# A gated attention unit followed by hash routing: the first z load, the place of the token load, one drain on GpSimd and the number of turns between two gates

## The chip, the cores and the metric

The kernel runs on one core of a Trainium2 chip. Its time is the device time of one execution in microseconds (us); smaller is better. The core has a matrix engine (PE, with its weight loads PEld), a vector engine (DVE), a scalar engine (ACT), GpSimd (POOL) and a sync engine (SP). SP, ACT and POOL can issue DMAs.

## The reference

Two stages run behind each other. In the first, for each of 8 batches of 2496 rows, with z of 64 columns and u, v of 256 columns:

```python
scores = scale * np.matmul(z, z.transpose(0, 2, 1))      # scale = 1 / 2496
attn = np.maximum(scores, 0.0) ** 2
out = np.matmul(attn, v)
x = u * out                                              # (8, 2496, 256)
```

In the second, each of the 19968 rows of x goes through the expert that its token id names (8 experts, 256 to 1024 to 256 columns):

```python
expert_idx = token_ids * np.int64(2654435761) % np.int64(E)
for e in range(E):
    h = np.maximum(x[expert_idx == e] @ w1[e], 0.0)
    out[expert_idx == e] = h @ w2[e]
```

## The kernel before, in words

**Tiles.** A batch has T = 20 tiles of rows: TM = 19 of 128 rows and one odd tile of 64 rows. A partition holds 19 neighbouring rows, so tile t is row t of each partition. Five groups (NG = 5) of G = 4 tiles form a batch; the last group has three whole tiles and the odd one.

**z.** The scores need z with its 64 columns on the partitions, and they need it twice, in partitions 0 to 63 and 64 to 127, because even and odd tiles use the two halves of PE at the same time (`scores`, line 202). For batch 0, `load_z` (line 121) loads z twice side by side, once from SP and once from ACT, and `turn_z` (line 149) turns each tile with its copy on PE with an identity matrix, four tiles into one PSUM tile, which one ACT copy takes to `zT`. In the later batches DVE turns z instead.

**Scores and squares.** `scores(b, g)` makes the scores of all tiles against the four tiles of group g. ACT and DVE take turns at the relu out of PSUM (batch 0: even tiles ACT, odd tiles DVE). `square(n)` squares the next n of them, on DVE in batch 0, on ACT later. PSUM has six buffers for scores and everything else of `mm_ps`, and two accumulators (`acc_ps`).

**Mirrored batches.** From batch 1 on the symmetry of the scores is used: only some tiles are computed, and DVE turns the others in 32x32 blocks (`turns_of`, line 236, and `own_turns`). These turns stand in a list `to_turn`, and `turn_scores(steps)` (line 275) sends out as many as 1600 elements per step allow, each costing its elements and 170. `turn_now` sends out at once what an attend needs and has not been turned.

**The order.** All of it is written by hand in one loop over the 40 groups (line 589). A group begins with the attends of its first EARLY = 2 tiles, goes on tile by tile (an attend of four matmuls, `square(2)`, `turn_scores(1)`, one small step of the routing by `between`), then makes the scores of the next group, and ends with two halves: the last LATE = 3 tiles for two of the four row tiles, their gates (`gate`, line 332: accumulator times u, on DVE), then `square(2)`, `turn_scores(1)`, `between`. A gate frees the accumulator that the next group begins with.

**Routing.** `places` computes on DVE, in steps between the attends, where each token goes; its first step reads the token ids. POOL then writes each row of x to its slot in DRAM by indirect DMAs.

**The experts.** Behind the loop, `run` (line 706) takes blocks of 256 slots: `up` (matmuls, relu), `down` (matmuls, ACT copy), and `store`, an indirect DMA from POOL. The last two blocks come behind a branch (`tc.If`, line 730) for a token distribution that needs more blocks; POOL issues twelve stores for that case (`later`) in any event, whose indices are out of bounds when the branch is not taken.

**Queues at the start.** SP issues its copy of z(0), V(0) in seven DMAs, u(0,0), and z(1) with V(1). ACT issues the other copy of z(0) and the token ids. POOL makes the constants: a corner of `short`, the identity, index tables, and `zero` (line 358), the source of the DMAs that clear the slots.

Of the kernel before, what the change touches and what calls it, by code (L numbers as in the profile page):

```python
# [10 lines left out]
F32 = mybir.dt.float32  # L11
# [13 lines left out]
def kernel(  # L25
# [59 lines left out]


    short = const.tile([P, T, R], F32)
    nc.gpsimd.memset(short[R:P, TM, :], 0.0)
    odd = const.tile([R, D], F32)
    ident = const.tile([P, P], F32)  # L90
    make_identity(nc, ident[:])

# [25 lines left out]

    def load_z(b):
        if b == 0:
            zn[b] = npool.tile([P, T, 2, K], F32, name="zn")
            for i in range(2):
                tiles_io(zf, b, range(T), zn[b][:, :, i, :], False, nc.scalar if i else nc.sync, twice=True)
            return
        zn[b] = npool.tile([P, T, NQ, Q], F32, name="zn")
        rows = zf[ds(b * S, S), :]
        for q in range(NQ):
            cols = ts(q % 2, Q)  # L130
            o = zn[b][ts(q, Q)]
            for t, m in ((slice(0, TM), rows[0:SM, cols].rearrange("(j i t) k -> i t j k", i=Q, t=TM)),
                         (TM, rows[SM:S, cols].rearrange("(j i) k -> i j k", i=Q))):
                if t == TM:
                    for h in range(2):
                        nc.sync.dma_start(o[:, TM, ds(h * R // Q, R // Q), :], m)
                else:
                    nc.sync.dma_start(o[:, t], m)
# [10 lines left out]
    def turn_z(b, g):  # L149
        if g == 0:  # L150
            zT[b] = zpool.tile([P, T * P], F32, name="zT")
        o = zT[b][:, ts(g, G * P)]
        if b:
            nc.vector.transpose(o, zn[b][:, ts(g, G)].rearrange("p t j k -> p (t j k)"))
            return
        ps = mm_ps.tile([P, G * P], F32, name="z_ps", tag="mm")
        for i, t in enumerate(group(g)):
            nc.tensor.transpose(ps[:, ts(i, P)], zn[b][:, t].rearrange("p h k -> p (h k)"), ident[:])
        nc.scalar.copy(o, ps[:])

    def whole(g):

# [34 lines left out]
    def scores(b, g):  # L197

        n = sum(width(t) for t in group(g))
        for k, t in enumerate(fresh(b, g)):  # L200
            lo = skipped(b, g, t)
            h = ds((t % 2 if t % G < 2 or not mirrored(b) else 1 - t % 2) * K, K)
            ps = mm_ps.tile([P, G * P], F32, name="s_ps", tag="mm")
            nc.tensor.matmul(ps[:, lo:n], zT[b][h, ts(t, P)], zT[b][h, ds(g * G * P + lo, n - lo)], start=True, stop=True)  # L204
            if t % G == 0:
                made[b, g, t // G] = apool.tile([P, G, G * P], F32, name="a", tag="a")
                rooms.append((b, g, t // G))
            a = made[b, g, t // G][:, t % G, lo:n]
            if (k % 8 == 7 and g < 2) if mirrored(b) else k % 2:
                nc.vector.tensor_scalar_max(a, ps[:, lo:n], 0.0)  # L210
            else:
                nc.scalar.activation(a, ps[:, lo:n], AF.Relu)  # L212
            to_square.append((b, g, t))

    def square(n):
        for b, g, t in to_square[:n]:
            a = made[b, g, t // G][:, t % G, :]
            m = len(whole(g)) * P
            lo = skipped(b, g, t)
            pairs = [(a[:, lo:m], a[:, lo:m])] if lo < m else []  # L220
            if m < G * P:
                pairs.append((short[0:width(t), t, :], a[0:width(t), ds(m, R)]))
            for o, x in pairs:
                if mirrored(b):
                    nc.scalar.square(o, x)  # L225
                else:
                    nc.vector.tensor_mul(o, x, x)
            if mirrored(b) and t % G == G - 1:
                turns = turns_of(b, g, t // G) if t // G > g else own_turns(b, g)
                to_turn.extend((n, (b, g, t // G), f) for n, f in turns)  # L230

                to_turn.sort(key=lambda e: min(e[1][2] - g, 2 if fine(g) else 1))
        del to_square[:n]
# [120 lines left out]
    token = const.tile([P, B, T], I32)  # L354

    tok = const.tile([P, B, T, 2], I32)
    zero = const.tile([P, D], F32)
    nc.gpsimd.memset(zero[:], 0.0)
    CLEAR = T // 2
    assert NS % CLEAR == 0  # L360

# [5 lines left out]
    def load_tokens():  # L367
        tok_h = dataclasses.replace(moe_token_ids.tensor, shape=list(moe_token_ids.tensor.shape))
        tok_w = tok_h.bitcast(I32).rearrange("(b s two) -> b s two", b=B, two=2)
        nc.scalar.dma_start(tok[:, :, 0:TM, :], tok_w[:, 0:SM, :].rearrange("b (p t) two -> p b t two", t=TM))  # L370
        nc.scalar.dma_start(tok[0:R, :, TM, :], tok_w[:, SM:S, :].rearrange("b p two -> p b two"))

    def places():

# [144 lines left out]
    def place_x():  # L519
# [5 lines left out]
        tc.declare_no_dep(st.ins, group="x", reason="each token has its own slot")  # L525
        tc.add_to_no_dep_group("x", st.ins)

    order = tc.manual_schedule()
    order.__enter__()

    load_z(0)
    load_v(0)
    load_u(0, 0)
    load_tokens()
    for g in range(NG):
        turn_z(0, g)

# [47 lines left out]
        nc.vector.transpose(xT[j].rearrange("p k h i -> p (k h i)"), xg[j].rearrange("p k d -> p (k d)"))  # L585

    scores(0, 0)
    square(EARLY)
    for n, (b, g) in enumerate(groups):
        if n + 1 < len(groups):  # L590
            load_u(*groups[n + 1])
        if g == 0 and b + 1 < B:
            load_z(b + 1)
            load_v(b + 1)
        if n == NG - 1:
            m = pool("mirror", 1)
            mirrors = [m.tile([P, G, G, P], F32, name=f"m_{k}") for k in range(NG * NG // 4)]

        acc = [acc_ps.tile([P, 2, D], F32, name="acc", tag="acc") for _ in range(2)]
        for k in range(2):  # L600
            for t in range(EARLY):
                attend(b, g, t, acc, [2 * k, 2 * k + 1])
            square(2)
            turn_scores(1)
            between()
        for t in range(EARLY, TM - LATE):
            if g == NG - 1 and b + 1 < B and t % 2 == 0 and t // 2 <= NG:
                turn_z(b + 1, t // 2 - 1)
            if n + 1 == len(groups) and t == T // 4:

                w_buf = list(mirrors)
                w_buf.extend(mirror[b, a, g] for a in range(NG - 1))
                load_w(0, 0)
            if n + 1 == len(groups) and t == T // 2:
                assert not gated
                x_all = vpool.tile([P, T, D], F32, name="v_sb")
                x_bufs = [x_all[:, ts(k, DP * BLK // D), :].rearrange("p c d -> p (c d)") for k in range(2 * LOADS)]
                xg_buf = [x.rearrange("p (k d) -> p k d", d=D // NQ) for x in x_bufs[:LOADS]]
                xT_buf = [x.rearrange("p (k h i) -> p k h i", h=DP, i=Q) for x in x_bufs[LOADS:]]
                for k in range(AHEAD):  # L620
                    load_x(k, k)
            if n + 1 == len(groups) and t >= TM - LATE - AHEAD:
                turn_x(t - (TM - LATE - AHEAD), t - (TM - LATE - AHEAD))
            attend(b, g, t, acc, range(G))
            if t % G == G - 1 and (b, t // G, g) in mirror and g < NG - 1:
                mirrors.append(mirror.pop((b, t // G, g)))
            square(2)
            turn_scores(1)
            between()
        assert not to_square  # L630
        if g == NG - 1:
            gate_short(b, attend_short(b))
            if n + 1 == len(groups):
                load_w(1, 1)
            mirrors.extend(mirror.pop(k) for k in sorted(mirror))
        attend_last(b, g, acc)
        between()
        if n + 1 < len(groups):

            m = len(fresh(*groups[n + 1])) // G  # L640
            for key in rooms[max(0, len(rooms) - NA):max(0, len(rooms) - NA + m)]:
                turn_now(key)
            scores(*groups[n + 1])
        square(3)
        turn_scores(1)

        for k in range(2):
            for t in range(TM - LATE, TM):
                attend(b, g, t, acc, [2 * k, 2 * k + 1])
            for q in (2 * k, 2 * k + 1):  # L650
                gate(b, g, q, acc)
            square(2)
            turn_scores(1)
            between()
        between()
    assert not to_turn and next(place, None) is None and i > 2 * T + 4 * C
# [49 lines left out]
    def run(first, last, loads, later=None):  # L706
# [19 lines left out]
    run(0, NM, NU)  # L726
    n_used = nc.values_load(extra[0:1, 0:1], min_val=1, max_val=NB + N, engines=[
        mybir.EngineType.PE, mybir.EngineType.Activation, mybir.EngineType.DVE, mybir.EngineType.SP])
    later = []
    with tc.If(n_used > NU):  # L730
        for j in [*range(AHEAD), *range(NU, NB)]:
# [37 lines left out]
```

## Time and profile before

| | |
|---|---|
| time, median of 3 runs | 2685.01 us (2684.61 to 2685.49) |
| the profiled execution's own time | 2687.06 us |
| its span, first to last instruction | 2685.1 us |
| PE, weight loads, DVE, ACT, POOL busy | 99%, 84%, 51%, 21%, 18% |
| first matmul starts, last one ends | 9.36 us, 2677.4 us |
| first scores, first attend | 13.79 us, 24.06 us |
| z loads of batch 0 issued | 0.82 us, from SP and ACT |
| token ids issued from ACT, first read on DVE | 4.42 and 8.27 us, 25.73 us |
| last store issued on POOL | 2678.05 us |

The page of a profile gives each engine's busy time and the costliest groups of instructions; the trace behind it can be asked for the waits (which engine waited for which, how long in total, how often, the longest), for a timeline of a window (start, duration, engine, line, operation, out and in, shapes, number, and in brackets the idle time before it with what ended it), for busy times in chosen stretches, and for the instructions of one line, the sequencers' own ones among them. Ends of matmuls are modelled, about 0.38 us behind the start for 256 columns, while the next starts 0.2155 us behind the last. A line number is that of the kernel.

### The profile page before, as it was taken

The numbers are of one execution on the slowest core, as the hardware profiler recorded it, in microseconds if no ns is written. First come the engines' busy times: TensorE is split into PE (matmuls) and PEld (weight loads), VectorE is DVE, ScalarE is ACT, GpSimd is POOL, SyncE is SP. The second block draws the span as 40 slices with busy tenths as digits, with TensorE's granted clock in tenths as the row PEclk, the third lists the DMA queues.
The fourth block names the chain that finished last, engine by engine and source line by source line (L and its number), as shares of the span: only waits on it lengthen the run. The fifth ranks groups of instructions, "written<-read, shape, count | busy, mean of one in ns | idle before, by whom it ended". The sixth has DMA issues, their size and how long they took to land. (4 is left out here: it accounts for less than half of the span.)

```text
span 2685.1 us, 33980 instructions
## 1 busy us (share of the span) xinstructions
PE 2662.1 (99%) x12650; PEld 2255.2 (84%) x12650; DVE 1357.5 (51%) x2813; ACT 567.6 (21%) x1221; POOL 494.2 (18%) x513
## 2 busy tenths in 40 slices
PE   8999999999999999999999999999999999999998
PEld 6877887888888888888878888888888888888887
DVE  6556886887878878878878811111111111111110
ACT  2013314214222233123132111111111111111111
POOL 0221222122212221222101121111111111111113
PEclk9999999999999999999999999999999999999999
DMA  9612113013103122131101287777777777777773
GB/s 295 206 31 74 32 32 89 17 32 89 31 20 87 31 46 62 29 90 32 32 16 32 62 200 188 187 188 193 195 187 190 188 187 186 194 194 192 188 189 88
DMA packets 334842, 308.93 MB, mean 115 GB/s; under 512 B 187308, under 2 KB 293693, under 8 KB 334672
## 3 DMA queue, kind: packets, MB, share of 16 engines
q1 hardware_dynamic: 309424, 264.78, 39.2%
q0 software_dynamic: 21072, 41.10, 5.2%
q8 instruction: 102, 1.67, 0.3%
q10 hardware_dynamic: 4176, 0.82, 0.2%
q14 instruction: 68, 0.56, 0.1%
HBM read 243.25 MB, written 65.70 MB: 115 GB/s over the span
## 5 line engine op out<-in xcount | busy, mean ns | idle before, releaser
L329 PE MATMUL acc<-v_sb,a 128*128 128x256 f32 x3760 | 828.7, 380 | 3.7 <-issue 2.2
L329 PEld LDWEIGHTS acc<-v_sb,a 128*128 128x128 f32 x3760 | 710.3, 190 | 112.5 <-issue 7.9
L241 DVE STREAM_TRANSPOSE m<-a 32x512 f32<-32x512 f32 (+1 forms) x1120 | 756.8, 676 | 17.1 <-issue 0.3
L683 DVE TENSOR_SCALAR hT<-h_ps 128x512 f32<-128x512 f32 x162 | 112.1, 692 | 951.0 <-PE h_ps L675 933.9
L675 PE MATMUL h_ps<-v_sb,m 128*128 128x256 f32 x2592 | 586.0, 379 | 2.2 <-issue 1.1
L688 PE MATMUL o_ps<-m,hT 128*128 128x256 f32 x2592 | 585.2, 379 | 0.0
L675 PEld LDWEIGHTS h_ps<-v_sb,m 128*128 128x128 f32 x2592 | 492.3, 190 | 70.3 <-issue 2.1
L688 PEld LDWEIGHTS o_ps<-m,hT 128*128 128x128 f32 x2592 | 492.5, 190 | 67.0
L329 PE MATMUL acc<-v_sb,m 128*128 128x256 f32 x2016 | 439.7, 379 | 0.0
L329 PEld LDWEIGHTS acc<-v_sb,m 128*128 128x128 f32 x2016 | 383.0, 190 | 52.1
L212 ACT ACTIVATE a<-s_ps 128x512 f32<-128x512 f32 (+3 forms) x442 | 205.7, 578 | 902.9 <-PE s_ps L204 902.9
L522 POOL DMA_INDIRECT x_rows<-x_sb,slot_i x160 | 157.8, 986 | 1075.4 <-DVE x_sb L338 884.8
L700 POOL DMA_INDIRECT out_dram<-o_sb,idx x158 | 153.5, 972 | 918.7 <-ACT o_sb L695 903.8
L695 ACT COPY o_sb<-o_ps 128x256 f32<-128x256 f32 x162 | 60.3, 372 | 741.4 <-PE o_ps L688 737.5
L204 PE MATMUL s_ps<-zT 64*128 64x512 f32 (+5 forms) x1040 | 211.2, 549 | 0.0
L257 DVE STREAM_TRANSPOSE a<-a 32x128 f32<-32x128 f32 (+2 forms) x896 | 201.4, 249 | 7.8
L225 ACT ACTIVATE a<-a 128x512 f32<-128x512 f32 (+3 forms) x413 | 202.1, 625 | 0.0
L204 PEld LDWEIGHTS s_ps<-zT 64*128 64x128 f32 x1040 | 123.9, 187 | 81.8 <-issue 57.2
L510 POOL DMA_INDIRECT slot_tokens<-token,addr x160 | 158.8, 993 | 159.4 <-DVE addr L504 109.1
L681 ACT ACTIVATE hT<-h_ps 128x512 f32<-128x512 f32 x162 | 96.7, 597 | 229.0 <-PE h_ps L675 218.2
L210 DVE TENSOR_SCALAR a<-s_ps 128x512 f32<-128x512 f32 (+1 forms) x78 | 51.4, 659 | 146.6 <-PE s_ps L204 145.5
L338 DVE SCALAR_TENSOR_TENSOR x_sb<-acc,u_sb 128x256 f32<-128x256 f32 x152 | 57.9, 420 | 133.7 <-PE acc L329 132.8
(80 smaller groups left out, 380.6 us busy)
## 6 DMA issues: line engine op xcount, KB each, us to landing
m<-in_moe_w_dram SPq DMA_DIRECT2D x324, 256.0 KB
m<-in_moe_w_dram SPq DMA_DIRECT2D x81, 1024.0 KB
x_rows<-zero SPq DMA_DIRECT2D x10, 2176.0 KB
v_sb<-x_rows SPq DMA_DIRECT2D x324, 64.0 KB
v_sb<-in_v_dram SPq DMA_DIRECT2D x32, 512.0 KB
u_sb<-in_u_dram SPq DMA_DIRECT2D x32, 512.0 KB
zn<-in_z_dram SPq DMA_DIRECT2D x28, 304.0 KB
v_sb<-in_v_dram SPq DMA_DIRECT2D x8, 384.0 KB
```

The lines of the kernel that those rows point to most:

```text
L204: nc.tensor.matmul(ps[:, lo:n], zT[b][h, ts(t, P)], zT[b][h, ds(g * G * P + lo, n - lo)], start=True, stop=True)
L212: nc.scalar.activation(a, ps[:, lo:n], AF.Relu)
L225: nc.scalar.square(o, x)
L241: nc.vector.transpose(mirror[b, a, g][ts(c, Q)].rearrange("p t s q -> p (t s) q")[:, 0:m, ts(r, Q)], made[b, a, g][ts(r, Q)].rearrange("p ...
L257: return n * Q, lambda: nc.vector.transpose(out, in_)
L329: nc.tensor.matmul(acc[i // 2][:, i % 2, :], lhs(b, g, t, i), v_sb[b][:, t, :], start=(k == 0 and i % 2 == 0), stop=(k == TM - 1), skip_gr ...
L510: st = nc.gpsimd.indirect_dma_start(out=slot_dram[:, None], out_offset=bass.IndirectOffsetOnAxis(ap=addr[0:n, c:c + 1], axis=0), in_=token ...
L522: st = nc.gpsimd.indirect_dma_start(out=x_dram[:, :], out_offset=bass.IndirectOffsetOnAxis(ap=slot_i[0:width(c % T), c:c + 1], axis=0), in ...
L675: nc.tensor.matmul(ps[:, i, :], w1[j][:, c, ts(f + i, P)], xT[j][:, :, c, :], start=(c == 0), stop=(c == DP - 1))
L683: nc.vector.tensor_scalar_max(o, ps[:], 0.0)
L688: nc.tensor.matmul(ps[:], hT[j][:, f, ts(t, P)], w2[j][:, f, :], start=(f == 0), stop=(f == FP - 1))
L700: st = nc.gpsimd.indirect_dma_start(out=out[:], out_offset=bass.IndirectOffsetOnAxis(ap=rows, axis=0), in_=o, in_offset=None, bounds_check ...
```

## The change

z of batch 0 is loaded once, from SP, in one piece of 19 rows per partition, with a slot 0 ahead of the tiles that gets a copy of the odd tile on DVE. Turning slots t and t + 1 together puts tile t - 1 in the lower half and tile t in the upper half; DVE copies the upper half to its place, ACT the lower half, one tile further on (for the first group in two pieces, since the odd tile goes to the end). `zero` is the first memset that POOL makes for the kernel; ACT makes a one-element copy of it first of all, and PE five matmuls with it into a PSUM tile that nobody reads. The token ids are loaded from SP, behind V(0) and ahead of u(0,0). In the scores of the very first group, the first two squares are made by ACT behind score 10 instead of by DVE behind score 19. `turn_scores` between the two halves at a group's end gets 0.8 steps instead of 1. POOL gets a drain instruction ahead of the branch to the last blocks.

```diff
     short = const.tile([P, T, R], F32)
-    nc.gpsimd.memset(short[R:P, TM, :], 0.0)
     odd = const.tile([R, D], F32)
+    zero = const.tile([P, D], F32)
+    nc.gpsimd.memset(zero[:], 0.0)
     ident = const.tile([P, P], F32)
     make_identity(nc, ident[:])
+    nc.gpsimd.memset(short[R:P, TM, :], 0.0)
...
         if b == 0:
-            zn[b] = npool.tile([P, T, 2, K], F32, name="zn")
-            for i in range(2):
-                tiles_io(zf, b, range(T), zn[b][:, :, i, :], False, nc.scalar if i else nc.sync, twice=True)
+
+            zn[b] = npool.tile([P, T + 1, K], F32, name="zn")
+            tiles_io(zf, b, range(T), zn[b][:, 1:, :], False, nc.sync, twice=True)
+            nc.vector.tensor_copy(zn[b][:, 0, :], zn[b][:, T, :])
             return
...
         for i, t in enumerate(group(g)):
-            nc.tensor.transpose(ps[:, ts(i, P)], zn[b][:, t].rearrange("p h k -> p (h k)"), ident[:])
-        nc.scalar.copy(o, ps[:])
+            nc.tensor.transpose(ps[:, ts(i, P)], zn[b][:, t:t + 2].rearrange("p t k -> p (t k)"), ident[:])
+        nc.vector.tensor_copy(o[K:P], ps[K:P, :])
+        for i, n in ((0, G), ) if g else ((0, 1), (1, G - 1)):
+            nc.scalar.copy(zT[b][0:K, ds((g * G + i - 1) % T * P, n * P)], ps[0:K, ds(i * P, n * P)])
...
             to_square.append((b, g, t))
-
-    def square(n):
+            if (b, g, t) == (0, 0, T // 2):
+                square(EARLY, nc.scalar)
+
+    def square(n, eng=None):
...
-                if mirrored(b):
+                if mirrored(b) or eng is nc.scalar:
                     nc.scalar.square(o, x)
...
-    zero = const.tile([P, D], F32)
-    nc.gpsimd.memset(zero[:], 0.0)
...
-        nc.scalar.dma_start(tok[:, :, 0:TM, :], tok_w[:, 0:SM, :].rearrange("b (p t) two -> p b t two", t=TM))
-        nc.scalar.dma_start(tok[0:R, :, TM, :], tok_w[:, SM:S, :].rearrange("b p two -> p b two"))
+        nc.sync.dma_start(tok[:, :, 0:TM, :], tok_w[:, 0:SM, :].rearrange("b (p t) two -> p b t two", t=TM))
+        nc.sync.dma_start(tok[0:R, :, TM, :], tok_w[:, SM:S, :].rearrange("b p two -> p b two"))
...
+    WARM = 5
...
+    nc.scalar.copy(odd[0:1, 0:1], zero[0:1, 0:1])
+    warm = mm_ps.tile([P, D], F32, name="warm", tag="mm")
+    for _ in range(WARM):
+        nc.tensor.matmul(warm[:], zero[:, 0:P], zero[:], start=True, stop=True)
     load_z(0)
     load_v(0)
+    load_tokens()
     load_u(0, 0)
-    load_tokens()
...
     scores(0, 0)
-    square(EARLY)
...
             square(2)
-            turn_scores(1)
+            turn_scores(1 if k else 0.8)
             between()
...
         mybir.EngineType.PE, mybir.EngineType.Activation, mybir.EngineType.DVE, mybir.EngineType.SP])
+
+    nc.gpsimd.drain()
     later = []
```

## The prediction, on record before the changed kernel ran

> **What bounds the kernel now.** I read the busy times first, then the waits of the matrix engine (PE), then the timeline where those waits lie.
>
> ```profile
> PE 2662.1 (99%) x12650; PEld 2255.2 (84%) x12650; DVE 1357.5 (51%) x2813; ACT 567.6 (21%) x1221; POOL 494.2 (18%) x513
> ```
>
> PE is busy for 2662.1 of 2685.1 us. The change takes no matmul out of the long loops, so it can only win in the 23 us where PE does not run, or where PE runs slower than it could. The waits of PE say where that is (us in total, times, longest):
>
> ```profile
> PE z_ps L158 <- DMA zn<-in_z_dram: 9.4, 1, 9.4
> PE acc L329 <- issue: 2.2, 7, 0.3
> PE acc L329 <- DVE a L227: 1.4, 1, 1.4
> PE h_ps L675 <- issue: 1.1, 3, 0.4
> PE h_ps L675 <- ACTq L730: 1.0, 1, 1.0
> ```
>
> These are 15.1 us; the rest is the 7.7 us behind the last matmul (2677.4 to 2685.1). Nothing else stands between this kernel and an unbroken matmul stream, so I go through the places that the edits touch.
>
> **The start.** Timeline, 0 to 40 us (start, duration, engine, line, operation):
>
> ```profile
> 0.82 5.47 SPq L113 DMA_DIRECT2D zn<-in_z_dram  x3
> 9.36 4.50 PE L158 MATMUL z_ps<-ident,zn 128*128 128x128 f32 x20 [9.36 <-DMA zn<-in_z_dram]
> 10.48 0.59 ACT L159 COPY zT<-z_ps 128x512 f32<-128x512 f32 x1 [0.25 <-PE z_ps L158]
> 11.33 0.59 ACT L159 COPY zT<-z_ps 128x512 f32<-128x512 f32 x1 [0.27 <-PE z_ps L158]
> 13.79 8.85 PE L204 MATMUL s_ps<-zT 64*128 64x512 f32 x40
> 23.32 2.49 DVE L227 TENSOR_TENSOR a<-a 128x512 f32<-128x512 f32 x4
> 24.06 12.35 PE L329 MATMUL acc<-v_sb,a 128*128 128x256 f32 x56 [1.42 <-DVE a L227]
> ```
>
> (1) The load. z(0) comes twice, in 256-byte pieces, by two queues; the stretches from 3.4 to 9.36 us show 223 to 228 GB/s. Now it comes once, 608 KB in one piece per partition and the odd tile twice at 16 KB: half of the bytes. A long-piece load that stands alone is u at 275.35: 512 KB, data from 276.3, at its end by 279.0, so 3.65 us from its issue, with 287 to 303 GB/s at the end. 640 KB add 128 KB at that rate, 0.45 us: 4.1 us, landing at 0.82 + 4.1 = 4.9. The odd tile's two small loads are issued behind it on SP and land inside that or a little later; the DVE copy that duplicates the odd tile waits for them. 128x64 lies between the rows 64x8 (0.16 us) and 128x152 (0.23 to 0.24 us). The first transpose can start near 5.2. If the small loads trail, 6.5; not before 4.9.
>
> (2) The warm-up. Five 128x256 matmuls are ten passes (the trace shows each fp32 matmul as two). Later passes run at 0.2155 us (48 in 10.52 at 2666.84, less one latency). PE needs `zero`, a 0.32 us memset now first on POOL, so it starts near 1.2 and ends at 3.4; at half pace at 5.5. It stands ahead of the transposes on PE; at worst it costs 0.3 us against the landing. I take 5.5 for the first transpose, 3.9 earlier than now.
>
> (3) The transposes. There are 20 as before. The ACT copies above come every 0.853 us for four transposes, 0.213 us for 128 columns: the price of a 256-column pass later. So they run at half the later pace per column, either because PE's clock is low after 9 idle us or because a transpose has that price. The granted clock in the windows reads 1.00 from 0 on, idle stretches included, so it does not decide. Bounds: 20 x 0.213 = 4.3 us if nothing changes, 20 x 0.107 = 2.1 us if PE is warm. I take a third at the old pace: 7 x 0.213 + 13 x 0.107 = 2.9. They end at 8.4 and, with the 0.33 us that PE loses at the switch, scores start at 8.7 instead of 13.79: **-5.1**; ends -2.7 (6.5 + 4.3 + 0.33 = 11.1) and -6.2 (5.2 + 2.1 + 0.33 = 7.6).
>
> [...]
>
> (4) The copies out of PSUM split: per group 0.69 us on DVE (the 128x512 rows of L210) beside 0.59 us on ACT, ACT with one more for the first group. Five on DVE take 3.5 us and end near 10. The first scores need only groups 0 and 1, ready near 8.0; the later buffers come free ahead of PE. Cost 0. The ACT table load (1.28 us at 8.95, behind ACT's DMA issues) goes to the first us, since ACT issues no DMA any more.
>
> (5) Squares 0 and 1 on ACT. PE waits 1.42 us for the first DVE square (23.32); at the next switch of the same kind (62.61) it waits for nothing. ACT now squares both tiles after score 10: 2 x 0.625 us ahead of the relus of scores 12 to 18. Pair j starts at 8.7 + 0.86j and its relu 1.16 us later (14.95 against 13.79), so score 10 is through ACT at 14.75, the squares at 16.0, score 12 at 16.6. Score 18 (j = 9, 16.4) takes the sixth buffer back, that of score 12: 0.28 us late. **-1.1** (ends -1.45 and -0.5). Next in line are squares 2 and 3 on DVE, due 3.4 us after the first attend and done 2 us after it.
>
> (6) Tokens. On SP behind seven V loads: issued near 7, behind 2.5 MB at 339 to 386 GB/s (30 to 50 us), landed by 14. Their first reader (DVE L400, 25.73 now) comes near 19.5. Cover 5 us; were it gone, DVE's squares queue behind it and PE waits one for one. u(0,0) moves 1.3 us back and is first read at 65.5; z(1), V(1) wait behind it with far more room. Cost 0. ACT's queue loses five DMA issues.
>
> Start: **-6.2**, ends -3.2 and -7.7.
>
> **The middle.** The seven waits of 0.3 us are one per batch, where its last group (three whole tiles, so one gate in the second half) meets the next. Timeline near 235 us:
>
> ```profile
> 232.18 0.76 DVE L338 SCALAR_TENSOR_TENSOR x_sb<-acc,u_sb 128x256 f32<-128x256 f32 x2 [3.39 <-PE acc L329]
> 232.85 2.12 DVE L241 STREAM_TRANSPOSE m<-a 32x512 f32<-32x512 f32 x3
> 235.00 0.42 DVE L338 SCALAR_TENSOR_TENSOR x_sb<-acc,u_sb 128x256 f32<-128x256 f32 x1
> 235.48 4.80 PE L329 MATMUL acc<-v_sb,a 128*128 128x256 f32 x21 [0.32 <-issue]
> ```
>
> Two gates, three turns of 0.7 us, then the third gate, and PE resumes 0.06 us after that gate ends: it needs the accumulator that the gate frees. Counting `turn_scores` by its own arithmetic (1600 per step, 682 per turn) gives three turns there now and two at 0.8, in all seven batches. The gate then ends at 234.72. The 26 passes from 229.28 would take 5.60 at 0.2155 and the next starts 6.20 later: 0.5 to 0.6 lost, more than the table's 0.32 since ends are modelled. PE would want the buffer at 235.0, so all of it goes: 7 x 0.54 = **-3.8**, ends 0 and -4.2. What is put off: at most seven small or three large turns; by the same count none is ever forced, and the tightest is emitted five steps (of 1.72 us) ahead of its attend, six now. Price if that cover is gone: rival 4.
>
> **The end.** Sequencer instructions of the last line (count, shortest/median/longest ns):
>
> ```profile
> L764 SPq DRAIN  x3: 7/7/13, 2681.5 to 2684.5; - x3
> L764 POOLq DRAIN  x3: 40/108/6432, 2677.8 to 2684.8; - x3
> ```
>
> POOL's first drain takes 6.43 us, until 2684.25; SP is through with its waits at 2681.5, so POOL's drain sets the last 2.7 us. The drains that follow it take 0.108 and 0.040 us, one after four memsets 0.19 us. So a drain costs what has piled up before it; here that is 494 indirect DMAs, and with a drain before the last 16 stores only those. Upper gain 2.7 (SP becomes the end), lower 0 (the cost hangs on the last store alone). Nearest are the cheap drains that follow a drain: I take **-2.0**. Below nothing: the new drain holds POOL for perhaps 6.4 us from 2648. Behind it stand 12 stores (1.28 us each, back to back) and four real ones; 2654.7 + 12 x 1.28 = 2670, and the last store issues at 2678.05 now. It stays hidden up to some 11 us. The stretch 2661.4 to 2666.8, where PE takes 5.4 us for 16 passes worth 3.4, has no named cause; I leave it (0, ends +2 and -2).
>
> **Sum.** -6.2 - 3.8 - 2.0 = -12.0. The profiled execution took 2687.06 (span 2685.1 and 1.96 around it), 2.05 above the median of the runs, 2685.01, about what that last stretch loses; so its absolute time is not that of the runs, but the places hold for both. 2687.06 - 12.0 = 2675.1 for a like profile; for the median **2673.0**. A measurement of this kernel tells 0.2% (5.4 us) from no change.
>
> **Rivals.**
> 1. The drain is fixed in cost: both drains long, the end as now. For: 3.8 us of the 6.43 lie behind the last store's landing. Against: 0.108 us for the next one. 2675.0. Chance 0.25.
> 2. The start gains little: the small z loads trail and the transposes keep 0.213 us. Start -3.2, end 0: 2685.0 - 3.2 - 3.8 = 2678.0. For: 0.213 may be the price of a transpose. Chance 0.12, a third of it within 0.2%.
> 3. The change doesn't do what it says in the middle: the third gate is still late, since PE's own order sets it. 2676.8, or 2678.8 with rival 1. Against: PE resumes 0.06 us behind the gate. Chance 0.09, half of it within 0.2%.
> 4. Slower: turns put off between gates come late. Each group boundary then has PE wait for one 0.70 us turn at the attend that reads the mirror; 35 groups x 0.7 = +24.5, so 2697.5. It decides from the point where DVE lags PE by five steps, 8.6 us; DVE is 80 to 82% busy from 700 to 1300 us. Against: apart from the seven, no wait of PE on a turn. Chance 0.05.
>
> Forecast 0.45; none of these, within 0.2%, 0.04. Faster 0.45 + 0.25 + 0.08 + 0.05 = 0.83, same 0.04 + 0.04 + 0.04 = 0.12, slower 0.05. The range goes from 2670.0 (start -7.7, middle -4.2, end -2.7 and a little) to 2678.5 (rivals 2 and 3).
>
> **What would show it.** The first transpose near 5.5 and scores near 8.7; transposes at 0.107 us once warm; no wait ahead of the first attend; two turns between gates at 234.8 less the shift and no 0.3 us waits; a POOL drain near 2637 and a short one at the end. Wrong if scores start after 10, if DVE L400 waits for tokens, if waits on L241 appear, or if the last POOL drain is still 6.4 us.

## The result, and the profile after

The changed kernel takes 2671.36 us (median of 6 runs, 2671.24 to 2672.65), the kernel before, measured beside it, 2684.91 us (2684.48 to 2685.49). The ratio is 0.9951, with a 95% interval of 0.9938 to 0.9963: 13.55 us less, where 12.0 had been forecast. The profiled execution took 2672.32 us, its span is 2670.6 us.

The engines of the profile after (busy us, share of the span, instructions):

```profile
PE 2662.6 (100%) x12660; PEld 2262.3 (85%) x12660; DVE 1362.9 (51%) x2817; ACT 568.4 (21%) x1225; POOL 494.7 (19%) x513
```

PE has ten passes more than before (the warm-up, 4.63 us) and is busy for 0.5 us longer, in a span that is 14.5 us shorter: its idle time went from 23.0 to 8.0 us. All the waits of PE after (total, times, longest):

```profile
PE h_ps L687 <- ACTq L744: 1.2, 1, 1.2
PE warm L543 <- POOL zero L90: 1.2, 1, 1.2
PE z_ps L163 <- issue: 0.4, 1, 0.4
PE s_ps L211 <- ACT zT L166: 0.2, 1, 0.2
```

The 9.4 us ahead of the first transpose, the 1.4 us ahead of the first attend and the seven waits of 0.3 us are gone. What is left is the 1.2 us until the zeros are there, 0.6 us around the transposes, the 1.2 us at the branch, and 4.9 us behind the last matmul. The start in the timeline of after:

```profile
1.18 4.63 PE L543 MATMUL warm<-zero 128*128 128x256 f32 x10 [1.18 <-POOL zero L90]
5.94 0.20 DVE L128 COPY zn<-zn 128x64 f32<-128x64 f32 x1 [5.94 <-DMA zn<-in_z_dram]
6.24 2.85 PE L163 MATMUL z_ps<-ident,zn 128*128 128x128 f32 x20 [0.42 <-issue]
9.33 8.95 PE L211 MATMUL s_ps<-zT 64*128 64x512 f32 x40 [0.24 <-ACT zT L166]
15.27 1.14 ACT L234 ACTIVATE a<-a 128x512 f32<-128x512 f32 x2
18.21 6.09 PE L338 MATMUL acc<-v_sb,a 128*128 128x256 f32 x27
20.13 0.23 DVE L407 TENSOR_SCALAR eid_i<-tok 128x152 int32<-128x152 int32 x1
```

Read it from the bottom: the first attend starts at 18.21 instead of 24.06 us, with nothing to wait for, since ACT had squared at 15.27. The token ids are read at 20.13 without a wait. The 20 transposes take 2.85 us instead of 4.50: the first four come every 0.213 us, the others every 0.109. But the first one starts at 6.24, 0.42 us after the warm-up, because DVE's copy of the odd tile could start only at 5.94. The DMA records say why: z's long load landed at 4.41 us, the odd tile's two small ones, issued behind it on SP, at 5.54.

A batch's end in the middle, after:

```profile
223.43 8.90 PE L338 MATMUL acc<-v_sb,a 128*128 128x256 f32 x40
226.33 0.76 DVE L347 SCALAR_TENSOR_TENSOR x_sb<-acc,u_sb 128x256 f32<-128x256 f32 x2 [3.38 <-PE acc L338]
227.00 1.41 DVE L250 STREAM_TRANSPOSE m<-a 32x512 f32<-32x512 f32 x2
228.44 0.42 DVE L347 SCALAR_TENSOR_TENSOR x_sb<-acc,u_sb 128x256 f32<-128x256 f32 x1
```

Two turns instead of three between the gates, and PE's 40 passes run on without a break. And the sequencer instructions of the last line (times, then shortest/median/longest ns, first and last start):

```profile
L778 POOLq DRAIN  x3: 46/108/3291, 2666.1 to 2670.3; - x3
L778 SPq DRAIN  x3: 7/7/13, 2669.7 to 2670.0; - x3
```

POOL's last drain takes 3.29 us instead of 6.43 and ends at 2669.40; SP is through with its waits at 2669.7 and now sets the end. The added drain ahead of the branch takes 5.16 us (2637.06 to 2642.22), beside PE's work.

Laid side by side, the two profiled executions give this (us; the last column is a second trace of the changed kernel, the control among the experiments):

| stretch | forecast | first trace | control |
|---|---|---|---|
| span's start to the first attend | -6.2 | -5.85 | -6.76 |
| first attend to the first matmul behind the branch | -3.8 | -3.92 | -4.09 |
| first matmul behind the branch to the last | 0 (ends +2, -2) | -1.94 | -1.94 |
| last matmul to the span's end | -2.0 | -2.78 | -2.77 |
| sum | -12.0 | -14.5 | -15.6 |

The third row is, as far as the runs tell, not the change's. The stretch of before in which PE lost some 2 us for no named cause is missing in these two traces, but it is there in most of the edits below, whatever was edited (see the last experiment). Without that row the sums are -12.5 and -13.6, beside -13.55 in the runs; the execution of the first trace, 2672.32 us, is itself 0.96 us slower than the median of its runs.

### The profile page after: what moved, and what is told of

Read it like the earlier page. It is cut to its first block, busy times and chain, and to the rows that moved or that the text cites. A ratio compares the mean times of both kernels' runs of the same rounds, so it can differ in the third digit from the quotient of the medians.

```text
span 2670.6 us, 34006 instructions
## 1 busy us (share of the span) xinstructions
PE 2662.6 (100%) x12660; PEld 2262.3 (85%) x12660; DVE 1362.9 (51%) x2817; ACT 568.4 (21%) x1225; POOL 494.7 (19%) x513
```

## The experiments

Each is an edit of the changed kernel, timed in three rounds beside the kernel before on the same chip. Three chips took part, and on two of them the kernel before is 1.6 to 1.7 us slower than on the third. So the last column, each time less that of the kernel before on its own chip, is the one to compare; the changed kernel itself has -13.70.

| edit | median us | before, same chip | ratio, 95% interval | difference |
|---|---|---|---|---|
| no added drain | 2676.28 | 2686.86 | 0.9960 (0.9946 to 0.9975) | -10.58 |
| no warm-up | 2674.28 | 2686.86 | 0.9953 (0.9937 to 0.9970) | -12.58 |
| a whole step of turns | 2677.61 | 2686.86 | 0.9965 (0.9952 to 0.9977) | -9.25 |
| first squares on DVE | 2674.74 | 2686.86 | 0.9956 (0.9939 to 0.9972) | -12.12 |
| z twice, as before | 2677.99 | 2686.74 | 0.9968 (0.9957 to 0.9980) | -8.75 |
| tokens from ACT | 2674.76 | 2686.74 | 0.9955 (0.9939 to 0.9972) | -11.98 |
| drain behind the 12 stores | 2673.19 | 2686.74 | 0.9950 (0.9933 to 0.9967) | -13.55 |
| odd tile from ACT | 2676.69 | 2686.74 | 0.9963 (0.9949 to 0.9977) | -10.05 |
| unchanged (control) | 2671.45 | 2685.15 | 0.9950 (0.9933 to 0.9966) | -13.70 |
| without the 12 stores | 2671.58 | 2685.15 | 0.9949 (0.9932 to 0.9966) | -13.57 |
| odd tile first, 4 warm-up matmuls | 2672.47 | 2685.15 | 0.9952 (0.9935 to 0.9969) | -12.68 |
| 0.8 steps at batch ends alone | 2671.89 | 2685.15 | 0.9950 (0.9934 to 0.9967) | -13.26 |

The intervals of the ratios (some 4 us either way) overlap, so the table alone separates few of these; each verdict below rests on the stretch of the trace that the edit touches, with the difference beside it. On the two slower chips a stretch that no edit was aimed at moves by 0.4 us from trace to trace (last experiment), so differences between rows that small decide nothing.

**The added drain taken out**

```diff
-    nc.gpsimd.drain()
```

> The changed kernel without the drain ahead of the last blocks. Theory (a drain clears what has piled up before it): POOL's drain at the very end goes from 3.29 us back to about 6.4, and the time rises by 2.7 us to about 2674.1. If the stretch in which PE lost 1.9 us near 2663 in the kernel before belongs to the missing drain as well, it comes back and the time is about 2676. Rival (the end costs what the last store costs, the shorter end has another cause): the last drain stays near 3.3 us and the time near 2671.4.

The last line's sequencer instructions in this run:

```profile
L777 POOLq DRAIN  x3: 40/108/6432, 2667.4 to 2674.4; - x3
```

The last drain is 6.43 us again, as in the kernel before, and 3.1 us come back in the runs (-10.58 against -13.70). So the early drain alone shortens the late one, and hides its own 5.16 us. The time is also the one that was expected if the stretch in which PE loses some 2 us belonged to the missing drain, and that stretch is indeed there again. But it is there too in the other edits on this chip, whose drain is in place, so that part of the expectation is not confirmed.

**The drain moved behind the twelve stores**

```diff
-    nc.gpsimd.drain()
     later = []
...
     for o, rows in later:
         store(o, rows)
+    nc.gpsimd.drain()
```

> The changed kernel with the drain behind the twelve stores that the branch may need, ahead of the last four. Theory (a drain's cost grows with what lies before it): the last drain, with 4 instead of 16 transfers since the drain before, is as long or up to 0.5 us shorter than 3.29 us; the moved drain itself takes 2.4 to 4.2 us behind its last store's landing. Time 2671.0 to 2671.5. Rival (what counts is how long ago the drain was, or that the stores of the branch are out of bounds): the last drain grows towards 6 us, 2674.

The last line's sequencer instructions in this run:

```profile
L778 POOLq DRAIN  x3: 46/108/2810, 2666.9 to 2671.1; - x3
```

The last drain now has four stores ahead of it since the other drain instead of sixteen, and takes 2.81 us; the moved one ends at 2657.93 and holds the next store until 2658.79, which nothing waits for. The time is the changed kernel's (-13.55 against -13.70): SP sets the end by now, so the 0.48 us saved on POOL buy nothing.

**A whole step of turns in all groups**

```diff
-            turn_scores(1 if k else 0.8)
+            turn_scores(1)
```

> The changed kernel with a whole step of turns between the halves again. Theory (the third turn delays the gate that frees the accumulator): three turns between the gates at each of the seven batch ends, seven waits of PE of 0.3 us in the table and 0.59 us each from start to start, time plus 4.1, 2675.5. Rival (PE's waits went because the earlier start shifted DVE against PE): no waits, 2671.4.

Its timeline at the batch's end that was shown above:

```profile
226.34 0.76 DVE L347 SCALAR_TENSOR_TENSOR x_sb<-acc,u_sb 128x256 f32<-128x256 f32 x2 [3.39 <-PE acc L338]
227.01 2.12 DVE L250 STREAM_TRANSPOSE m<-a 32x512 f32<-32x512 f32 x3
...
229.16 0.42 DVE L347 SCALAR_TENSOR_TENSOR x_sb<-acc,u_sb 128x256 f32<-128x256 f32 x1
...
229.64 2.64 PE L338 MATMUL acc<-v_sb,a 128*128 128x256 f32 x11 [0.32 <-issue]
```

The third turn is back, the gate is 0.72 us later, and PE waits until 0.06 us after it. There are seven such places, 190 us apart, each with 0.70 us between two matmuls instead of 0.2155. The runs lose 4.45 us (-9.25 against -13.70).

**0.8 steps at the ends of batches alone**

```diff
-            turn_scores(1 if k else 0.8)
+            turn_scores(0.8 if g == NG - 1 and k == 0 else 1)
```

> The changed kernel with 0.8 steps of turns only between the two halves of each batch's last group, and a whole step between the halves of all other groups, as before the change. Theory A (the gain of the middle comes from the seven batch ends alone, where one gate stands behind three turns): no gap of 0.7 us, total that of the control within 0.6 us. Rival B (fewer turns between gates help in the other groups too, where PE loses nothing that the profile shows): 1 us or more above the control, with PE's time for a batch longer than in the control's trace.

PE runs through the batch end without a break (40 passes from 223.34), and the time is 0.44 us above the control, within what was allowed for. So the gain lies at the seven batch ends; 0.8 steps in the other groups of these batches are worth nothing that shows here.

**The first two squares back on DVE**

```diff
-            if (b, g, t) == (0, 0, T // 2):
-                square(EARLY, nc.scalar)
...
     scores(0, 0)
+    square(EARLY)
```

> The changed kernel with the first two squares back on DVE behind all scores. Theory (PE waited for the first square alone): PE waits 1.4 us again ahead of the first attend, which starts near 19.6 instead of 18.21; time plus 1.4, 2672.8. Rival (something else is late there now, V or the copies): the first attend stays near 18.2, 2671.4.

The first attends in the timeline of this run:

```profile
18.59 1.78 PE L336 MATMUL acc<-v_sb,a 128*128 128x256 f32 x7 [1.38 <-DVE a L234]
```

PE waits 1.38 us for DVE's square again. From the first score to the first attend it takes 10.34 us, against 8.88 in both traces of the changed kernel: 1.46. The runs lose 1.58 us.

**z loaded and turned as before**

```diff
+            for i in range(2):
+                tiles_io(zf, b, range(T), zn[b][:, :, i, :], False, nc.scalar if i else nc.sync, twice=True)
...
+            nc.tensor.transpose(ps[:, ts(i, P)], zn[b][:, t].rearrange("p h k -> p (h k)"), ident[:])
+        nc.scalar.copy(o, ps[:])
```

> The changed kernel with z loaded twice in 256-byte pieces by SP and ACT and turned as before, all else as changed. Theory (the load sets the start): the first transpose at 9.3 us or a little earlier, since the tokens no longer share the way, so 3.1 us later than in the changed kernel. The warm-up matmuls end at 5.8, 3.5 us ahead of it, so the clock may be low again: transposes at 0.213 and another 1.5 us. Time plus 3 to 4.8, 2674.4 to 2676.2. Rival (the halved bytes do not matter, the shared way with the tokens did): first transpose near 7, plus 1.

The PE rows of its first 22 us:

```profile
1.18 4.64 PE L541 MATMUL warm<-zero 128*128 128x256 f32 x10 [1.18 <-POOL zero L90]
9.25 3.96 PE L163 MATMUL z_ps<-ident,zn 128*128 128x128 f32 x20 [3.43 <-DMA zn<-in_z_dram]
13.14 8.89 PE L209 MATMUL s_ps<-zT 64*128 64x512 f32 x40
```

The first transpose starts at 9.25 us, near the 9.36 of the kernel before and 3 us later than with z in one piece, and the warm-up is mostly wasted: PE idles 3.43 us, the first five transposes still come every 0.109 us, and the others take 0.213 us again. The trace's clock records say so directly: full clock at 6.41, half at 9.83, full at 13.24. The loss is 4.95 us in the runs, the largest of any single part. The edit brings back the double bytes, the 256-byte pieces and the second queue together; no run tells which of them the 3 us belong to.

**No warm-up**

```diff
-    WARM = 5
+    WARM = 0
```

> The changed kernel without the five warm-up matmuls. Theory (PE's clock is low after idling, the matmuls open it): the first transpose starts near 6.1 us as now, but all 20 keep 0.213 us, scores start near 10.7 instead of 9.33, and the time rises by about 1.4 us to 2672.8. Rival (the transposes are faster for their new shape or place, not for the clock): 16 of 20 still at 0.11 us, scores near 9.2, time 2671.4 or a little less.

PE's first two rows in the timeline of this run:

```profile
6.38 4.32 PE L163 MATMUL z_ps<-ident,zn 128*128 128x128 f32 x20 [6.38 <-DVE zn L128]
10.63 8.85 PE L211 MATMUL s_ps<-zT 64*128 64x512 f32 x40
```

They begin at 6.38 us, no earlier than with the warm-up (6.24 and 5.61), so it costs next to nothing ahead of them: they start 0.30 us behind the start of DVE's copy here and in the first trace, 0.43 in the control. Now all 20 take 0.213 us, the first scores come at 10.63 instead of 8.42 to 9.33, and the runs lose 1.12 us. So 0.213 us is not the price of a transpose but of a PE ahead of its full clock, which the records of this trace show from 10.38 us on.

**Token ids from ACT, as before**

```diff
     load_v(0)
-    load_tokens()
     load_u(0, 0)
+    load_tokens()
...
-        nc.sync.dma_start(tok[...
+        nc.scalar.dma_start(tok[...
```

> The changed kernel with the token ids loaded from ACT as before. Theory (moving the tokens matters little once z comes in long pieces): the tokens' short pieces go out beside z and V, z lands up to 0.5 us later, the start moves by 0 to 0.5 us, time 2671.4 to 2671.9. Rival (the tokens' place is a main part of the gain): first transpose later by 1 us or more, 2672.5 and up.

ACT has no DMA ahead of them any more, so it issues them at 1.17 and 1.63 us. The transposes in the timeline of the profiled execution:

```profile
7.83 4.50 PE L163 MATMUL z_ps<-ident,zn 128*128 128x128 f32 x20 [2.01 <-issue]
```

The tokens' 1024 pieces of 152 bytes move from 3.76 to 5.06 us, their 512 pieces of 8 bytes from 4.50 to 6.96; the odd tile's pieces start at 4.34 instead of 3.75 and land at 6.94 instead of 5.54. So the first transpose is 1.6 us later than in the first trace, and PE, idle for 2.01 us, is cold to the last one (full clock at 13.72). This was the slowest run of the four (2677.68; the others begin at 2674.06), so the median's loss, 1.72 us, is for starts less bad than this one.

**The odd tile's two loads from ACT**

```diff
-            tiles_io(zf, b, range(T), zn[b][:, 1:, :], False, nc.sync, twice=True)
+            tiles_io(zf, b, range(TM), zn[b][:, 1:, :], False, nc.sync)
+            tiles_io(zf, b, [TM], zn[b][:, T:, :], False, nc.scalar, twice=True)
```

> The changed kernel with the odd tile's two small loads issued from ACT instead of behind the long load on SP. Theory (the last thing that the first transpose waits for is the DVE copy of the odd tile, whose loads land 1.1 us behind the long one): DVE's copy starts near 4.8 instead of 5.94, PE goes from the warm-up straight to the transposes, scores start 0.4 to 0.5 us earlier, near 8.9; time 2670.9. Rival (the small loads land late by the queue's way of working, whoever issues them): no change, 2671.4.

PE's transposes in the timeline of this run:

```profile
8.09 2.37 PE L164 MATMUL z_ps<-ident,zn 128*128 128x128 f32 x20 [2.28 <-issue]
```

A miss. A queue of their own did not bring the small loads forward: issued at 1.17 us, their first packet moves at 4.99 and the last lands at 7.03, among V's large ones, while z's long load still lands at 4.41. The first transpose starts at 8.09, and the runs lose 3.65 us. The trace is that of the fastest of five executions (2675.34 us; the others begin at 2676.52), so it does not show all of the loss.

**The odd tile's loads ahead of the long one, four warm-up matmuls**

```diff
-            tiles_io(zf, b, range(T), zn[b][:, 1:, :], False, nc.sync, twice=True)
+            tiles_io(zf, b, [TM], zn[b][:, T:, :], False, nc.sync, twice=True)
+            tiles_io(zf, b, range(TM), zn[b][:, 1:, :], False, nc.sync)
...
-    WARM = 5
+    WARM = 4
```

> The changed kernel with the two small loads of the odd tile issued ahead of the long load on SP's queue, and four warm-up matmuls instead of five. In the changed kernel the long load landed near 4.4 us and the small ones, issued behind it, at 5.5 us; issued from ACT they came later still. Theory A (the small loads trail because they are issued last on the queue): now they land with or ahead of the long load, which comes two issues later (1.1 to 1.3 us by SP's rows), so the data is there near 5.0 to 5.5 us, the warm-up ends near 5.0 us, the first transpose starts at 5.3 to 5.8 us instead of 6.24 and scores at 8.4 to 9.0 us instead of 9.3; total 0.3 to 0.8 us less than the control. Rival B (small pieces take their time wherever they stand): the first transpose stays at 6.2 us or comes later, and the total is that of the control within 0.5 us.

DVE's copy of the odd tile and PE's transposes in its timeline:

```profile
3.50 0.81 DVE L129 COPY zn<-zn 128x64 f32<-128x64 f32 x1 [3.50 <-DMA zn<-in_z_dram]
6.19 4.50 PE L164 MATMUL z_ps<-ident,zn 128*128 128x128 f32 x20 [1.23 <-DMA zn<-in_z_dram]
```

A second miss: the copy is early, the transposes are not. The small loads do land first (3.07 us), but the long one's first packet moves at 3.29 instead of 1.86 and its last lands at 5.73: the 1.4 us are only passed on. And the shorter warm-up leaves PE idle for 1.23 us and cold, with 0.213 us for every transpose and full clock at 10.80. The time is 1.0 us above the control in the median, but two of the four executions (2671.78 and 2671.81) lie 0.3 to 0.4 above it and two (2673.13 and 2673.44, the traced one) 1.7 to 2.0; none gains what was expected.

**The changed kernel again, and without the twelve stores**

The second one leaves the stores of the rows of the branch out:

```diff
-    for o, rows in later:
-        store(o, rows)
```

> The changed kernel itself, unchanged, run beside the other three on the same chip, so that a part can be read against the whole. Expected: ratio to the kernel before 0.9951, as in the first comparison (0.9938 to 0.9963); first transpose near 6.2 us, scores near 9.3 us, first attend near 18.2 us, drains of POOL near 5.2 and 3.3 us. Theory A (the gaps of PE behind the branch, some 1.3 to 2 us in the trace of before and of all experiments so far, belong to POOL's run of twelve stores with indices out of bounds): they are there again near 2661 us, and their absence in the first trace of the changed kernel was that execution's luck. Rival B (the changed kernel as a whole takes them away): PE runs unbroken from the branch to its last matmul, as in the first trace.

> The changed kernel without the twelve stores that stand behind the branch (left out: the rows that only the branch would make; with these inputs the branch is not taken and their indices are out of bounds). Theory A (these stores cause PE's gaps near 2661 us): no gap of PE over 0.3 us between the branch and the last matmul; 1.3 to 2 us less than the control where the control has the gaps, so some 2671.5 beside 2673.5. Rival B (the gaps come with the branch itself, for example with the code behind it, some 17 to 24 us behind it): the gaps stay where they were, and the time is that of the control within 0.5 us. In both cases the last drain of POOL stays near 3.3 us, if it pays for what lies between the two drains, or falls a little, since only four stores lie there instead of sixteen.

These were to say where the 2 us of before between 2661 and 2667 come from. From the first matmul behind the branch to the last takes 29.4 us, from start to start, in before's trace and 29.0 to 29.4 us in the traces of the first eight edits of the table, which ran on two chips; it takes 27.5 us in the first trace of the changed kernel and in the four traces of the third chip, with and without the twelve stores. So the pair could not tell the two theories apart: the control had nothing to take away. PE's rows of the stretch and one of ACT, in the timeline of the run with the moved drain:

```profile
2651.00 2.75 PE L687 MATMUL h_ps<-v_sb,m 128*128 128x256 f32 x12
2654.50 0.38 PE L687 MATMUL h_ps<-v_sb,m 128*128 128x256 f32 x1 [0.75 <-issue]
2655.21 0.91 PE L687 MATMUL h_ps<-v_sb,m 128*128 128x256 f32 x3 [0.33 <-issue]
2655.39 0.37 ACT L707 COPY o_sb<-o_ps 128x256 f32<-128x256 f32 x1 [4.47 <-remote]
2655.96 1.24 PE L700 MATMUL o_ps<-m,hT 128*128 128x256 f32 x5
```

and PE's in the timeline of the control:

```profile
2650.61 3.62 PE L687 MATMUL h_ps<-v_sb,m 128*128 128x256 f32 x16
2654.06 3.19 PE L700 MATMUL o_ps<-m,hT 128*128 128x256 f32 x14
```

The same 16 passes take 4.96 us in the one and 3.45 us in the other. PE is not alone in this: ACT's copy, which comes at 2650.81 us in the control, comes 4.2 us later here, measured against PE's rows, behind a wait that the profile puts down to no engine and no DMA of the kernel ("remote"); in each trace with the gaps ACT or DVE has such waits there, in none without them. On the two chips that have the gaps, the kernel before takes 2686.7 to 2686.9 us, on the third 2685.15; that fits gaps of 1.7 us that both kernels have or both lack. The one trace of the kernel before has the gaps, and its execution (2687.06 us) is as slow as those on the two chips. What remains of a link with POOL's stores is a matter of time only: without a drain ahead of them (before, the edit without it, and the one with the drain moved) the gaps begin 17 to 18 us behind the start of PE's wait at the branch; with a drain ahead of them they begin 24 to 25 us behind it, later by somewhat more than the drain takes (5.1 to 5.4 us). The cause stays open. The traces show that the gaps come and go while the code of that stretch stays the same: edits of the start and of the turns have them on two chips and not on the third. The changed kernel itself was not run on those two, so that these 2 us are not the change's is inferred from this and from the times of the kernel before, not shown by a pair. Without the twelve stores the last drain takes 2.85 us instead of 3.29, and the time is the control's.

## Why the prediction was right, step by step

**The start, -6.2: right in sum** (-5.85 and -6.76; the seven traces that leave the start as it is have the first attend between 17.30 and 18.22 us, 17.87 on average, which is -6.2). That the sum is met to a tenth is luck: over these seven the scores start at 8.99 us on average, 0.3 later than forecast, and the way from there to the first attend is 0.3 us shorter than forecast.

- The load was faster than worked out and its tail slower: the long piece landed at 4.41 instead of 4.9, but the small ones trailed by 1.1 us (0.5 in the control), so the first transpose came at 6.24 and 5.61 instead of 5.5. That they "land inside that or a little later" is the part that failed; 6.5 had been kept as the bound for it. Of the 0.91 us between the two traces 0.63 lie here (the small loads landed at 5.54 and 4.77); the rest are transposes ahead of the full clock, which came at 7.24 and 6.01.
- The transposes: 0.109 us once warm, as said; none to four at 0.213 us instead of seven. What 0.213 us stands for, which the trace of before left open, the edit without warm-up settles; the clock record of before's trace agrees, full from 13.76 us, where its transposes end. The five warm-up matmuls ended at 5.82 where "half pace" gave 5.5. With five of them the clock opened (first record of full clock) between 4.18 and 7.24 us in ten of eleven traces; with four it opened at 10.80, and with the tokens from ACT at 13.72. The gap behind the warm-up does not decide this alone: with the odd tile from ACT it was 2.28 us and the clock opened at 6.23, inside the gap, with the tokens from ACT it was 2.01 us and the clock stayed closed.
- When the clock opens is in part chance, as far as the traces tell. The records of the run with z as before go from full to half and to full again in two steps of the same size: from 6.41 to 9.83 and from there to 13.24 are 3.41 us each. In every trace the clock records lie 3.41 us or a whole multiple of it apart (full clock lasted 2665.81 us in before's trace and 2662.40 in the first trace of the changed kernel, 781 and 780 times 3.413), and the first one at another place in each trace. If the steps are counted back ahead of the first record, where no record stands (an estimate from these distances), the one that opened the clock held at most 0.62 us without a matmul; those ahead of it, which left it closed, held 0.62 (the first of the run with four matmuls) to 3.41 us. So a fixed number of cold transposes was the wrong thing to forecast. Transposes alone were enough to open it: in the run without warm-up full clock came at 10.38 us, with nothing but transposes on PE from 6.38 on.
- The squares gave -1.39 (10.27 to 8.88 us from first score to first attend), not -1.1: the 0.28 us by which score 18 was to be late are not there. The 40 matmuls of the scores take 8.95 us in place of 8.85, so 0.1 at most.
- The tokens were put at nothing, and only their own reader was looked at, which indeed waits for nothing. But left on ACT they cost 1.7 us in the runs, and in the trace they move among z's small pieces. The step holds for the change as made; what it gains was not seen.
- The single edits of the start add up to 9.4 us, more than the 5.9 to 6.8 that the start gained, as a late z also wastes the warm-up.

**The middle, -3.8: right.** -3.92 and -4.09 in the traces, 4.45 by the runs of the edit with whole steps. Up to the branch, whose own wait was 0.2 us longer in the first trace, the shift is 4.11, or 0.59 for each of seven. The table of waits showed 0.32 for each, since ends are modelled; the 0.54 worked out from the distance of starts was nearer. No put-off turn was late (rival 4), and the gate was what PE waited for (against rival 3).

**The end, -2.0: right in kind, short in size.** It gave -2.8, the upper end. "A drain costs what has piled up before it" holds in part only: 478 indirect DMAs taken from in front of it shorten the drain by 3.14 us, 12 more by 0.44 to 0.48, and with four left it still takes 2.8 us. Rival 1 (a fixed cost) is right about that remainder and wrong about the time: the remainder is over before SP is through.

**The unnamed stretch, 0 with ends of 2: right to leave alone.** As far as the runs show, it goes with the chip or the execution, not with the change. The remark that before's profiled execution is slower than its runs by about this stretch fits: the difference is 2.05 us, the stretch 1.94.

**The sum.** The 1.5 us between -12.0 and -13.55 are 0.8 at the end and 0.1 to 0.3 in the middle. The rest, some 0.5 us, lies within what the start moves from one execution to another, and of before's start only one trace exists.

## What to carry to other kernels

When a matrix engine is busy 99% of the time, list the places where it waits, and price each by the distance between two starts; here three lists of idle time (start, batch ends, end) gave the whole result to within 1.5 us. Look at what moves around a short load that a first instruction needs: here it trailed the long load on the same queue (5.54 us against 4.41 in the first trace), came later still from another engine's (7.03), and came early (3.07) only while the long load came later (5.73 instead of 4.41). A warm-up should end where the real work begins: with five matmuls and at most 1.0 us of gap behind them it opened the clock in every trace, with gaps of 2.0 to 3.4 us, one trace each, it opened and stayed open, opened and closed again, or did not open. Before comparing two profiles, see whether a stretch differs that neither edit touches: here some 2 us of the 14.5 between the two traces belong, as far as the runs tell, to neither kernel.

## What the runs showed of the hardware

- POOL's drain behind indirect DMAs took 2.81 and 2.85 us with 4 of them since the drain before, 3.29 with 16, 5.12 to 5.40 with 478 (the added one, ahead of the branch) and 6.43 with 494 (at the end); it does not grow in proportion.
- Two loads of 64 pieces of 256 bytes, 16 KB each, landed 0.5 to 1.3 us after a load of 608 KB in pieces of 4864 bytes that was issued just ahead of them (nine traces with the token ids behind V and the first z in one piece), 2.6 us after it with the token ids moving at the same time on ACT's queue, and 2.6 us after it when issued from ACT's queue themselves, with the same bytes.
- The records of PE's clock lay whole steps of 3.41 us apart, at a place that differed from trace to trace. Counted back ahead of the first record (an estimate), it went to full behind steps with at most 0.62 us without a matmul, and not behind steps with 0.62 us (four matmuls) and more; once open, it stayed open over a step with 1.86 us without one (odd tile from ACT, transposes at 0.109 us) and closed behind one with 2.83 us (z as before) and behind one with 2.20 us (before's end: last matmul to 2677.37, half clock from 2679.56). The limits in between were not tried, and the ends of matmuls in these figures are modelled.
